# Low parts of weights all on VectorE, the down-sampled norms and most output copies on ScalarE

## The chip, the cores and the metric

The kernel runs on one core of a Trainium2 chip. The metric is the device time of one execution in microseconds (us). Times of the kernel before: 1001.62 us median of 3 runs (1001.51 to 1006.58). The profiled execution, from which all durations below come, took 1001.4 us, of which 999.3 us lie between its first and its last instruction (the span). Engines are named as the profile names them: PE is TensorE (PEld its weight loads), DVE VectorE, ACT ScalarE, POOL GpSimd, SP the engine that issues most DMAs.

## The reference

Attention on 4 batches of 8 heads, 576 positions, 64 wide, and behind it two feed-forward stages on all 2304 positions (tokens) of width 512:

```
q_d, k_d, v_d = means over 4 neighbours of q, k, v          # 144 positions per head
out_up        = repeat(softmax(q_d k_d^T / 8) v_d, 4)       # the down-sampled branch
out_local     = softmax(q k^T / 8 where |i-j| < 4) v        # a window of 7 positions
x = (out_up + out_local) as [2304, 512]
x = (silu(x @ w_gate) * (x @ w_val)) @ w_out                # 512 -> 1536 -> 512
h = x @ w_in;  x = (h * clip(h + 3, 0, 6) / 6) @ w_out2     # 512 -> 2048 -> 512
```

The weights arrive as 64-bit numbers. Products are made from two parts of each factor, a high part (the value rounded to PE's fp32r format) and a low part (what the rounding left): high by high, low by high and high by low are summed.

## The kernel before

**Blocks.** The 2304 tokens are cut into five blocks of 8, 6, 8, 8 and 6 units of 64 tokens (512 or 384 columns); they are called block 0 to 4. Each block runs through 68 weight tiles of 128x512, called units too: first, in the G half, 12 of `w_gate` (PSUM tile pG), 12 of `w_val` (pV) and 12 of `w_out` (aO), in the order G0 G1 V0 V1 G2 G3 V2 V3 O0 O1 G4 ...; then, in the H half, 16 of `w_in` (pH) and 16 of the second `w_out` (aP), two and two. A unit of G, V or H is 12 matmuls (4 row tiles by 3 products).

**Weights.** Block 0 loads each tile from the input, puts the 64-bit number together and writes it back to a scratch tensor `kept`; the later blocks load pairs of tiles from `kept` (w<-kept, three buffers). `split_unit` then makes the two parts of a tile, two units ahead of the unit that PE works on, into one of four `wr` buffers: ACT copies the high part (line 228), and line 231 subtracts it from the weight. That subtraction is on DVE, except in block 1, where every fourth tile's is on POOL (`POOL_SPLIT`, 17 tiles).

**Attention beside it.** Batch 0 is done ahead of the blocks. For batches 1 to 3 it is spread over the blocks: in the G half of block bi the window scores of chunks (DVE, lines 781 and 784, 2 us each), in the H half the window values (lines 818 to 824), whose result PE transposes (px, line 838) and DVE adds to the down-sampled branch (line 847). The down-sampled branch of batch bi+1 is made in blocks 0 to 2: POOL sums four neighbours (line 290 the first addition, line 291 the second, into the tiles dnq, dnk, dnv: four sums each, of half the positions by half the heads), PE transposes dnq and dnk (pqT and pkT, line 303, copied by ACT on line 314), and in the H half `down_main` goes through the heads: scores on PE (pS), maximum on DVE (line 697), exponential with its sum on ACT (line 701), the norm in `norm_d` (lines 707 to 709, all on DVE), a transpose on PE (pPT, line 715), a copy on ACT, the product with the values on PE (pO, line 722).

**What sets the order.** Each engine runs its own instructions strictly in the order of its list; semaphores make it wait where an operand comes from another engine. The lists are made by a scheduler when the program is built: it starts from the order of the program text and from its own idea of what each instruction takes, and puts forward what it believes to be ready. The only fixed order is that of instructions marked `keep_in_program_order`. So a change of an engine or of an operation can move other instructions too. The input DMAs and the output DMAs all stand in SP's one list.

**Outputs.** At the end of a block `put_out` copies each finished 128x512 tile of aP out of PSUM, the even ones on ACT (line 1014), the odd ones on DVE (line 1012), and SP sends it off (line 1023).

Of the kernel before, what the change touches and what calls it, by code (L numbers as in the profile page):

```python
# [10 lines left out]
F32 = mybir.dt.float32  # L11
# [6 lines left out]
AF = mybir.ActivationFunctionType  # L18
ALU = mybir.AluOpType
# [14 lines left out]
CLOAD = (0, 4)  # L34

EARLY = 6

POOL_SPLIT = {1: 4}


@with_exitstack
def tile_kernel(
# [12 lines left out]
    nc = tc.nc  # L55
# [6 lines left out]
    NJ = S // 4  # L62
    NJH = NJ // 2
# [10 lines left out]
    NB = len(BLOCKS)  # L74
# [44 lines left out]
    def flat(ap, off, dims):  # L119
        return bass.AP(ap.tensor, ap.offset + off, dims)  # L120
# [7 lines left out]
    def behind(ins):  # L128

        if front[0]:  # L130
            tc.keep_in_program_order(ins)
# [5 lines left out]
    units = []  # L137
# [20 lines left out]
    def view(t, i):  # L158
        return t[:, i % 2, :].rearrange("p (c e) -> p c e", c=NC)
# [65 lines left out]
    def split_unit(i):  # L225
        s = view(w32[i // 2], i)
        r = sp.tile([P, 2, NC, P], F32R, tag="wr", name=f"wr{i}", bufs=4)
        behind(nc.scalar.activation(r[:, 0], s, AF.Copy))  # L228
        n = POOL_SPLIT.get(units[i][2])
        eng = nc.gpsimd if n and i % n == 0 else nc.vector  # L230
        behind(eng.tensor_tensor(r[:, 1], s, r[:, 0].bitcast(F32), op=ALU.subtract))  # L231
        split[i] = r

    def prefetch(i):
        steps = ((LR, load_raw), (LD, load_kept), (LA, decode_a), (LB, decode_b), (LS, split_unit))
        for ahead, fn in steps:
            if 0 <= i + ahead < len(units):
                fn(i + ahead)
# [467 lines left out]
    def norm_d(pd, sd):  # L706
        nc.vector.tensor_scalar(sd, sd, EPS, 4.0, op0=ALU.add, op1=ALU.mult)
        nc.vector.reciprocal(sd, sd)
        nc.vector.tensor_tensor(pd, pd, sd[:, :, None].to_broadcast([NJH, 2, NJ]), op=ALU.mult)

    def trans_d(pd, ps):
        pt = ps[:NJH, :2 * NJ].rearrange("p (g j) -> p g j", g=2)
# [292 lines left out]
    def put_out(bi, e, ps):  # L1005
        if e == 0:

            done = sp.tile([P, NC, 2, UMAX * UT], F32R, tag="x2", name=f"os{bi}", bufs=1).bitcast(F32)
            state["os"] = done.rearrange("p c a t -> p (c a t)")
        os = state["os"][:, e * DM:(e + 1) * DM]  # L1010
        if e % 2:
            nc.vector.tensor_copy(os, ps)
        else:
            nc.scalar.activation(os, ps, AF.Copy)
        gu = starts[bi] + 2 * e
        (b, u), (b1, _) = divmod(gu, NG), divmod(gu + 1, NG)
        for n, m in ((0, 2),) if b == b1 else ((0, 1), (1, 1)):
            b, u = divmod(gu + n, NG)
            if b == 0:
                dst = out[(gu + n) * UT:(gu + n + m) * UT, :]  # L1020
            else:
                dst = flat(out, (b * S + u * 4) * DM, [[DM, 4 * m], [SL * DM, NSEG], [1, DM]])
            nc.sync.dma_start(dst, os[n * UT:(n + m) * UT, :])
# [115 lines left out]
```

## Time and profile before

| | before |
|---|---|
| median of 3 runs | 1001.62 us |
| the profiled execution | 1001.4 us, span 999.3 us |
| PE busy | 955.3 us (96%) |
| DVE busy | 787.6 us (79%) |
| ACT busy | 510.6 us (51%) |
| POOL busy | 137.2 us (14%) |

The five blocks begin at 72.8, 274.1, 453.4, 660.0 and 849.8 us of the span. How to read the rows further below: a row of a group of instructions gives line, engine, operation, tile written <- tiles read, shape, count, then busy time and mean duration in ns, then the idle time of that engine just before them and who ended it. A row of the timeline gives start and length in us. Two instructions of one engine can overlap a little, so that the distance of two starts (the pitch) is somewhat less than the duration. In the rows by stage (windows) each engine's busy time in the stretch is followed by its count, and PEclk is the granted clock of PE: 1.00 is 2.4 GHz, 0.50 would be 1.2 GHz throughout.

### The profile page before, as it was taken

The numbers are of one execution on the slowest core, as the hardware profiler recorded it, in microseconds if no ns is written. First come the engines' busy times: TensorE is split into PE (matmuls) and PEld (weight loads), VectorE is DVE, ScalarE is ACT, GpSimd is POOL, SyncE is SP. The second block draws the span as 40 slices with busy tenths as digits, with TensorE's granted clock in tenths as the row PEclk, the third lists the DMA queues.
The fourth block names the chain that finished last, engine by engine and source line by source line (L and its number), as shares of the span: only waits on it lengthen the run. The fifth ranks groups of instructions, "written<-read, shape, count | busy, mean of one in ns | idle before, by whom it ended". The sixth has DMA issues, their size and how long they took to land.

```text
span 999.3 us, 13482 instructions
## 1 busy us (share of the span) xinstructions
PE 955.3 (96%) x4800; PEld 796.1 (80%) x4800; DVE 787.6 (79%) x1251; ACT 510.6 (51%) x1058; POOL 137.2 (14%) x130
## 2 busy tenths in 40 slices
PE   8769999999998999879999999999999999999997
PEld 5658888778797987767878777788888788999996
DVE  6698986899999879998985699999346995545653
ACT  4667566766543475444333654443335444544653
POOL 5680000000068211103630000000000000000000
PEclk9789999999999999999999999999999999999999
DMA  9979999377677532245753212354322233533331
GB/s 194 211 222 318 304 321 319 115 248 262 222 238 219 179 107 80 85 148 164 222 172 115 76 64 93 124 191 141 104 85 90 85 100 111 157 125 124 124 123 50
DMA packets 83655, 160.72 MB, mean 161 GB/s; under 512 B 19460, under 2 KB 51716, under 8 KB 83588
## 3 DMA queue, kind: packets, MB, share of 16 engines
q1 hardware_dynamic: 78692, 142.03, 45.4%
q10 hardware_dynamic: 4896, 17.83, 5.1%
q8 instruction: 38, 0.62, 0.3%
q14 instruction: 29, 0.24, 0.1%
HBM read 137.29 MB, written 22.54 MB: 160 GB/s over the span
## 4 chain that ended last, share of the span: by engine, by line
PE 78%; DVE 14%; ACT 2%; issue 2%; DMA 2%; SPq 0%; ACTq 0%; DVEq 0%
PE aP L989 19%; PE pH L947 19%; PE aO L989 13%; PE pG L947 12%; PE pV L947 11%; DVE wr L231 3%; DVE pr L781 2%; DVE sc L784 1%; PE pS L872 1%; DVE gV L965 1%; ACT held L561 1%; PE pO L722 1%; DMA w<-kept 1%; DVE sl L959 1%; DMA w<-in_moe_w_val_dram 1%
## 5 line engine op out<-in xcount | busy, mean ns | idle before, releaser
L231 DVE TENSOR_TENSOR wr<-w,wr 128x512 fp32r<-128x512 f32 x323 | 235.1, 731 | 106.3 <-ACT wr L228 104.7
L228 ACT ACTIVATE wr<-w 128x512 fp32r<-128x512 f32 x340 | 212.1, 626 | 170.5 <-PE aP L989 58.7
L947 PE MATMUL pH<-x,wr 128*128 128x512 f32 (+1 forms) x960 | 217.2, 376 | 4.2 <-DVE wr L231 4.2
L989 PE MATMUL aP<-wr,gH 128*128 128x512 f32 x864 | 216.9, 400 | 0.7 <-DVE wr L231 0.7
L947 PEld LDWEIGHTS pH<-x,wr 128*128 128x128 f32 x960 | 173.6, 188 | 33.0 <-DVE wr L231 5.5
L989 PEld LDWEIGHTS aP<-wr,gH 128*128 128x128 f32 x864 | 160.5, 189 | 38.4 <-issue 2.3
L947 PE MATMUL pG<-xr,wr 128*128 128x512 f32 (+3 forms) x732 | 158.9, 371 | 10.8 <-ACT xr L265 4.2
L989 PE MATMUL aO<-gV,wr 128*128 128x512 f32 (+1 forms) x720 | 157.8, 375 | 2.9 <-DVE wr L231 2.9
L947 PEld LDWEIGHTS pG<-xr,wr 128*128 128x128 f32 x732 | 133.9, 192 | 30.4 <-ACT xr L265 4.3
L947 PE MATMUL pV<-xr,wr 128*128 128x512 f32 (+1 forms) x720 | 153.1, 368 | 0.0
L989 PEld LDWEIGHTS aO<-gV,wr 128*128 128x128 f32 x720 | 132.8, 190 | 22.7 <-DVE wr L231 3.6
L947 PEld LDWEIGHTS pV<-xr,wr 128*128 128x128 f32 x720 | 131.0, 188 | 16.7
L962 ACT ACTIVATE h<-pH,half 128x512 f32<-128x512 f32 (+1 forms) x80 | 51.6, 645 | 75.8 <-PE pH L947 75.5
L963 DVE SCALAR_TENSOR_TENSOR h<-h,pH 128x512 f32<-128x512 f32 (+1 forms) x80 | 50.4, 631 | 25.1 <-ACT h L962 24.0
L953 ACT ACTIVATE sl<-pG 128x512 f32<-128x512 f32 (+1 forms) x60 | 33.2, 554 | 64.6 <-PE pG L947 64.3
L964 ACT ACTIVATE gV<-sl 128x512 fp32r<-128x512 f32 (+1 forms) x60 | 35.2, 587 | 57.5 <-DVE sl L959 56.8
L781 DVE TENSOR_TENSOR pr<-q,k 128x1792 f32<-128x1792 f32 x27 | 58.8, 2178 | 6.7 <-DMA k<-in_k_dram 6.7
L231 POOL TENSOR_TENSOR wr<-w,wr 128x512 fp32r<-128x512 f32 x17 | 23.2, 1363 | 288.6 <-DVE h L963 195.2
L208 ACT ACTIVATE top<-w 128x512 f16<-128x512 bf16 x68 | 53.0, 790 | 10.4 <-DMA w<-in_moe_w_in_dram 4.0
L964 ACT ACTIVATE gH<-h 128x512 fp32r<-128x512 f32 (+1 forms) x80 | 46.9, 587 | 19.3 <-DVE h L963 17.3
L965 DVE TENSOR_TENSOR gH<-h,gH 128x512 fp32r<-128x512 f32 (+1 forms) x80 | 51.9, 650 | 3.6 <-ACT gH L964 2.6
L818 DVE TENSOR_TENSOR pv<-sc,v 128x1792 f32<-128x1792 f32 x27 | 54.5, 2018 | 0.2
(128 smaller groups left out, 825.1 us busy)
## 6 DMA issues: line engine op xcount, KB each, us to landing
w<-kept SPq DMA_DIRECT2D x136, 512.0 KB
kept<-w ACTq DMA_DIRECT2D x34, 512.0 KB
w<-in_moe_w_out_dram SPq DMA_DIRECT2D x28, 512.0 KB
w<-in_moe_w_in_dram SPq DMA_DIRECT2D x16, 512.0 KB
w<-in_moe_w_gate_dram SPq DMA_DIRECT2D x12, 512.0 KB
w<-in_moe_w_val_dram SPq DMA_DIRECT2D x12, 512.0 KB
out_dram<-os SPq DMA_DIRECT2D x16, 256.0 KB
nq<-in_q_dram SPq DMA_DIRECT2D x12, 288.0 KB
```

The source lines that it names most:

```text
L208: behind(nc.scalar.activation(halves(top[i % 2], 2, F16)[:, :, 1], h3.bitcast(BF16), AF.Copy))
L228: behind(nc.scalar.activation(r[:, 0], s, AF.Copy))
L231: behind(eng.tensor_tensor(r[:, 1], s, r[:, 0].bitcast(F32), op=ALU.subtract))
L781: nc.vector.tensor_tensor(pr, qt[:, a:a + SUB, None, :].to_broadcast([P, SUB, W, D]), win(kt, a, SUB), op=ALU.mult)
L818: nc.vector.tensor_tensor(pr, pe[:, a:a + SUB, :, None].to_broadcast([P, SUB, W, D]), win(vt, a, SUB), op=ALU.mult)
L947: nc.tensor.matmul(ps[:, cs], r[:, a, c], x[:, c, b_, cs], start=part is HIGH and a == c == 0, stop=part is LOW and c == NC - 1,)
L953: nc.scalar.activation(sl, ps, AF.Silu)
L962: nc.scalar.activation(h, ps, AF.Relu, scale=1 / 6, bias=half1[:, 0:1])
L963: nc.vector.scalar_tensor_tensor(h, h, 1.0, ps, op0=ALU.min, op1=ALU.mult)
L964: nc.scalar.activation(g[:, 0, :nt], h, AF.Copy)
L965: nc.vector.tensor_tensor(g[:, 1, :nt], h, g[:, 0, :nt].bitcast(F32), op=ALU.subtract)
L989: nc.tensor.matmul(ps, **one, start=f_ == 0 and a == b_ == 0, stop=f_ == nf - 1 and b_ == 1,)
```

## The change

POOL no longer makes any low part; `norm_d` keeps the two small operations on the sums on DVE and lets ACT multiply, in two instructions per head, one for each half of the positions; ACT copies all outputs, except that in the last block the odd ones stay on DVE.

```
-POOL_SPLIT = {1: 4}
...
-        n = POOL_SPLIT.get(units[i][2])
-        eng = nc.gpsimd if n and i % n == 0 else nc.vector
-        behind(eng.tensor_tensor(r[:, 1], s, r[:, 0].bitcast(F32), op=ALU.subtract))
+        behind(nc.vector.tensor_tensor(r[:, 1], s, r[:, 0].bitcast(F32), op=ALU.subtract))
...
         nc.vector.reciprocal(sd, sd)
-        nc.vector.tensor_tensor(pd, pd, sd[:, :, None].to_broadcast([NJH, 2, NJ]), op=ALU.mult)
+        for half in range(2):
+            nc.scalar.activation(pd[:, half], pd[:, half], AF.Copy, scale=sd[:, half:half + 1])
...
-        if e % 2:
+        if e % 2 and bi == NB - 1:
             nc.vector.tensor_copy(os, ps)
```

In the lists, POOL loses 17 instructions, all in block 1. Here is POOL's list at the start of block 1, before (names carry the program's numbers: wr72 is the buffer of tile 72, nq2_00 the q input of batch 2, first half of the positions and of the heads):

```order
L231 TENSOR_TENSOR wr68_2797<-w32_68_2706,wr68_2797 128x512
L290 TENSOR_TENSOR nq2_00_2877<-nq2_00_2877 72x4x128
L291 TENSOR_TENSOR dnq2_2874<-nq2_00_2877 72x256
L231 TENSOR_TENSOR wr72_2887<-w32_72_2795,wr72_2887 128x512
L290 TENSOR_TENSOR nq2_01_2879<-nq2_01_2879 72x4x128
L291 TENSOR_TENSOR dnq2_2874<-nq2_01_2879 72x256
```

and now (line numbers are 3 or 4 lower):

```order
L286 TENSOR_TENSOR nq2_00_2885<-nq2_00_2885 72x4x128
L287 TENSOR_TENSOR dnq2_2882<-nq2_00_2885 72x256
L286 TENSOR_TENSOR nq2_01_2887<-nq2_01_2887 72x4x128
L287 TENSOR_TENSOR dnq2_2882<-nq2_01_2887 72x256
L286 TENSOR_TENSOR nq2_10_2891<-nq2_10_2891 72x4x128
```

The sums of the down-sampled inputs now stand on POOL with nothing between them. The second place is PE's list at the start of block 2, before (pG2_2 is G2 of block 2, pqT3_0 the first transposes of dnq for batch 3):

```order
L947 MATMUL pV2_1_4651<-xr2_3832,wr139_4597 128x512 x12
L947 MATMUL pG2_2_4683<-xr2_3832,wr140_4628 128x512 x12
L947 MATMUL pG2_3_4705<-xr2_3832,wr141_4648 128x512 x12
L947 MATMUL pV2_2_4729<-xr2_3832,wr142_4674 128x512 x12
L947 MATMUL pV2_3_4749<-xr2_3832,wr143_4702 128x512 x12
```

and now:

```order
L944 MATMUL pV2_1_4667<-xr2_3844,wr139_4613 128x512 x12
L944 MATMUL pG2_2_4699<-xr2_3844,wr140_4644 128x512 x12
L299 MATMUL pqT3_0_5186<-ident_96,dnq3_4631 128x72 x4
L944 MATMUL pG2_3_4721<-xr2_3844,wr141_4664 128x512 x12
L944 MATMUL pV2_2_4745<-xr2_3844,wr142_4690 128x512 x12
```

The four transposes of pqT3_0, which stood 252 matmuls later, between V7 and O4 (units of block 2), now stand behind G2. They read the first and the third of the four sums in dnq. All other small PE groups (pS, pPT, pO, px, the other pqT and pkT) have moved by 12 matmuls at most. The third place is ACT's list at the start of block 1's H half, before (pd2_0 is the softmax tile of batch 2, head 0; h1_1, gH1_1 the activation of unit H1; wr109 the tile of unit P1, which is the second of aP):

```order
L701 ACTIVATE pd2_1_3719,sd2_1_3720<-pS2_1_3684,nm2_1_3717 72x144 x2
L964 ACTIVATE gH1_1_3705<-h1_1_3706 128x384
L228 ACTIVATE wr109_3777<-w32_108_3614 128x512
L962 ACTIVATE h1_2_3754<-pH1_2_3740,half1_101 128x384
```

and now:

```order
L697 ACTIVATE pd2_1_3727,sd2_1_3728<-pS2_1_3692,nm2_1_3725 72x144 x2
L961 ACTIVATE gH1_1_3713<-h1_1_3714 128x384
L706 ACTIVATE pd2_0_3721<-pd2_0_3721,sd2_0_3722 72x144 x2
L706 ACTIVATE pd2_1_3727<-pd2_1_3727,sd2_1_3728 72x144 x2
L959 ACTIVATE h1_2_3764<-pH1_2_3750,half1_101 128x384
L697 ACTIVATE pd2_2_3771,sd2_2_3772<-pS2_2_3731,nm2_2_3769 72x144 x2
L697 ACTIVATE pd2_3_3777,sd2_3_3778<-pS2_3_3732,nm2_3_3775 72x144
L961 ACTIVATE gH1_2_3763<-h1_2_3764 128x384
L697 ACTIVATE pd2_3_3777,sd2_3_3778<-pS2_3_3732,nm2_3_3775 72x144
L706 ACTIVATE pd2_2_3771<-pd2_2_3771,sd2_2_3772 72x144 x2
L706 ACTIVATE pd2_3_3777<-pd2_3_3777,sd2_3_3778 72x144 x2
L226 ACTIVATE wr109_3789<-w32_108_3622 128x512
```

The new norms (line 706) stand directly behind the exponentials, and the high part of wr109 has moved behind four exponentials and eight norms.

## Rows read from the trace of the kernel before

**Rows 1.** The page: the span, and part 1, PE.

```profile
span 999.3 us, 13482 instructions
...
PE 955.3 (96%) x4800; PEld 796.1 (80%) x4800; DVE 787.6 (79%) x1251; ACT 510.6 (51%) x1058; POOL 137.2 (14%) x130
```

**Rows 2.** Windows of half blocks; columns us, PE, PEld, DVE, ACT, POOL, PEclk, DMA, GB/s.

```profile
274.10:359.10 85.00, 78.86 (x450) 77.63 (x449) 75.79 (x80) 36.09 (x69) 44.24 (x33) 0.98 0.65 207
359.10:453.40 94.30, 84.56 (x451) 68.82 (x450) 88.83 (x180) 50.42 (x124) 9.52 (x7) 0.98 0.30 100
453.40:557.80 104.40, 101.58 (x449) 81.76 (x448) 81.60 (x88) 39.46 (x69) 32.92 (x24) 1.00 0.54 165
557.80:660.00 102.20, 102.15 (x498) 78.78 (x497) 96.14 (x184) 54.63 (x124) 0.00 (x0) 1.00 0.29 97
660.00:758.90 98.90, 98.90 (x433) 81.06 (x433) 62.46 (x79) 39.13 (x65) 0.00 (x0) 1.00 0.38 125
758.90:849.80 90.90, 90.90 (x398) 73.16 (x397) 74.84 (x128) 44.40 (x77) 0.00 (x0) 1.00 0.29 95
849.80:925.10 75.30, 75.30 (x434) 75.30 (x433) 39.32 (x64) 35.35 (x65) 0.00 (x0) 1.00 0.43 138
```

**Rows 3.** Groups by line, POOL, 266 to 453 us: the low parts in block 1.

```profile
L231 POOL TENSOR_TENSOR wr<-w,wr 128x512 fp32r<-128x512 f32 x17 | 23.2, 1363 | 288.6 <-DVE h L963 195.2 <-ACT wr L228 79.4 <-PE pPT L715 14.0
```

**Rows 4.** Timeline of POOL, block 1, H half.

```profile
374.01 1.30 POOL L231 TENSOR_TENSOR wr<-w,wr 128x512 fp32r<-128x512 f32 x1 [10.26 <-ACT wr L228]
```

**Rows 5.** Timeline of DVE, block 1: two low parts; a norm of sc.

```profile
343.69 1.28 DVE L231 TENSOR_TENSOR wr<-w,wr 128x512 fp32r<-128x512 f32 x2
...
374.23 1.15 DVE L813 TENSOR_TENSOR sc<-sc,sm 128x56 f32<-128x56 f32 x1
```

**Rows 6.** Groups by line and form, DVE, 359 to 453 us.

```profile
L231 DVE TENSOR_TENSOR wr<-w,wr 128x512 fp32r<-128x512 f32 x25 | 18.0, 723 | 0.2 <-ACT wr L228 0.2
...
L965 DVE TENSOR_TENSOR gH<-h,gH 128x384 fp32r<-128x384 f32 x16 | 10.2, 634 | 0.2
...
L823 DVE TENSOR_TENSOR pv<-pv 128x512 f32<-128x512 f32 x8 | 6.1, 761 | 0.0
L709 DVE TENSOR_TENSOR pd<-pd,sd 72x288 f32<-72x288 f32 x8 | 3.6, 444 | 0.0
...
L813 DVE TENSOR_TENSOR sc<-sc,sm 128x56 f32<-128x56 f32 x4 | 2.9, 716 | 0.0
```

**Rows 7.** The same view, block 4 (850 to 999 us): gH without POOL.

```profile
L965 DVE TENSOR_TENSOR gH<-h,gH 128x384 fp32r<-128x384 f32 x16 | 8.9, 558 | 0.0
```

**Rows 8.** Same view, block 2 (557 to 660 us): sc without POOL.

```profile
L813 DVE TENSOR_TENSOR sc<-sc,sm 128x56 f32<-128x56 f32 x1 | 0.2, 208 | 0.0
```

**Rows 9.** Timeline of PE, block 1, G half: a wait for POOL, one for DVE.

```profile
311.36 4.28 PE L947 MATMUL pG<-xr,wr 128*128 128x384 f32 x23 [2.06 <-POOL wr L231]
...
324.95 3.59 PE L989 MATMUL aO<-gV,wr 128*128 128x384 f32 x11 [2.86 <-DVE wr L231]
```

**Rows 10.** Windows: PE behind the wait that ends at 324.95 us.

```profile
326.00:329.00 3.00, 3.00 (x13) 0.66 0.96 327
```

**Rows 11.** Timeline of SP, start of block 2: the first inputs of batch 3.

```profile
457.02 2.09 SPq L124 DMA_DIRECT2D nq<-in_q_dram  x2
```

**Rows 12.** Timeline of POOL, start of block 2: the third sum of dnq.

```profile
473.75 1.07 POOL L291 TENSOR_TENSOR dnq<-nq 72x256 f32<-72x256 f32 x1
```

**Rows 13.** Timeline of PE, start of block 2: G2, then G3.

```profile
464.00 2.88 PE L947 MATMUL pG<-xr,wr 128*128 128x512 f32 x12
468.98 2.97 PE L947 MATMUL pG<-xr,wr 128*128 128x512 f32 x12 [2.10 <-DVE sl L959]
```

**Rows 14.** Chain of waits, 430 to 560 us: the first pqT of block 2.

```profile
528.93 0.25 PE pqT L303 x4
```

**Rows 15.** Groups by line, ACT: its nearest row to a norm of one half.

```profile
L463 ACT ACTIVATE qdT<-tmp 128x144 f32<-128x144 f32 x4 | 1.3, 321 | 0.9 <-DVE tmp L460 0.8
```

**Rows 16.** Timeline of DVE, block 0: between two steps of a norm.

```profile
194.38 2.01 DVE L818 TENSOR_TENSOR pv<-sc,v 128x1792 f32<-128x1792 f32 x1
```

## The prediction

> **What bounds the kernel now.** I read the page first, then the stages, then who waits, then the lists. PE is busy for 955.3 of 999.3 us [rows 1], so at most 44 us can go without taking work from PE. The windows by half block [rows 2] (block 1 G and H, block 2 G and H, block 3 G and H, block 4 G) say where the rest is. In block 3 and in block 4's G half PE has no idle time at all, though DVE has a good deal (62.46 of 98.90 us busy): nothing that DVE gives up there moves the end. Block 2's H half is the same to 0.1 us of PE (102.15 of 102.20), although DVE is at 94%. Block 1 is the exception: PE is idle for 6.1 us of its G half (85.00 - 78.86) and 9.7 us of its H half (94.30 - 84.56), while DVE is busy for 75.8 of 85.0 and 88.8 of 94.3 us. There DVE sets the pace. Block 2's G half sits between: PE idles 2.8 us (104.40 - 101.58), and it takes 5.5 us more than block 3's, which has the same matmuls. So an edit counts where it changes DVE's load in block 1, or makes PE wait anywhere.
>
> **Low parts from POOL to DVE.** Seventeen subtractions of 1.36 us leave POOL [rows 3], seven of them in block 1's H half (POOL x7 in [rows 2]) and ten before. DVE pays for each not its 0.68 us duration but its pitch: two in a row take 1.28 us [rows 5], so the second costs 0.60. That is 17 x 0.60 = 10.2 us more for DVE. But POOL's work was not free to DVE. A norm of sc, which takes 0.21 us where POOL rests [rows 8], took 1.15 at 374.23 us and ended at 375.38 [rows 5], just behind POOL's subtraction, which ended at 375.31 [rows 4]. In block 1's H half POOL does nothing but these seven, so the lengthening of DVE's rows there is their price: low parts 25 x (0.723 - 0.68) = 1.1, gH 16 x (0.634 - 0.558) = 1.2, line 823 (as large as a low part) 8 x (0.761 - 0.68) = 0.6, sc 4 x (0.716 - 0.208) = 2.0, together 5.0 us or 0.71 each [rows 6 to 8]. Against 0.60 that is a relief of 0.11 each: 0.8 us in the H half, 1.1 in the G half. So the move costs DVE nothing, where a count of busy time would say 10 us.
>
> The Trainium skill ("SBUF — State Buffer", section "SBUF: two separate sides") says that GpSimd and a VectorE instruction with two SBUF inputs take a shared port pair exclusively for a whole instruction. The end of the sc norm agrees. Were DVE shut out for all of each subtraction, 1.36 us, the relief would be 17 x 0.76 = 12.9 instead of 1.9 us, and the forecast 11 us lower; I keep the rows' 0.71, since DVE's reductions and its reads of PSUM go on.
>
> **Norms and output copies.** Per block 0 to 2, eight multiplications of 0.44 us [rows 6] leave DVE, at the same overlap 0.36 each, 2.9 us. In blocks 0 and 2 PE is the bound and they buy nothing; in block 1's H half they count. Of the seven copies that leave DVE two stand at the start of block 1's G half, 2 x 0.60 = 1.2 us; the others lie beside a full PE.
>
> **Block 1, summed.** H half: relief 0.8 + 2.9 = 3.7 us. If DVE stays as full as it is, 94.3 x (88.8 - 3.7) / 88.8 = 90.4, 3.9 us less; I take 3.5, because ACT's part below is in the way. G half: relief 1.1 + 1.2 = 2.3 us, and PE's wait for a POOL subtraction that stood behind a sum, 2.06 us [rows 9], ends with its cause: 4.4. The wait of 2.86 us for DVE [rows 9] would be shorter too. Behind it PE's granted clock was 0.66 [rows 10], a mixture of 1.2 and 2.4 GHz, and 11 matmuls took 3.59 us where 23 of the same shape take 4.28 [rows 9]: 3.59 - 11 x 0.186 = 1.5 us for the fallen clock. I count hardly any of that: 4.5. Block 1 together: -8.0, with -3 as the least (POOL's wait and 1 us more) and -14 as the most (G's whole idle time, its 1.5 us, and two thirds of H's).
>
> **Block 2: the transposes that moved.** The new list has PE do the first pqT behind G2. In the run before they were done at 528.93 us [rows 14], long after their sums. Now PE comes to them when G2 ends, 464.00 + 2.88 = 466.9 [rows 13], but the third sum, which they need, ends at 473.75 + 1.07 = 474.8 [rows 12]. It cannot come much sooner: SP sends for q at 457.02 [rows 11], behind block 1's outputs, in an order that the change leaves alone here, and moves with the end of block 1. With the transposes' 0.25 us [rows 14] G3 starts at 475.1 instead of 468.98 [rows 13], where it already waited 2.10 for DVE: +6.1. Everything behind stands in PE's list and waits too. After 8 us without work I add the fallen clock of [rows 10], +1.5. Something comes back: of the 5.5 us over block 3, 2.1 are that old wait and 1.0 the four groups of transposes; the other 2.4 are later waits for DVE, which can run ahead while PE stands. I take 1.6 of them back. Block 2: 6.1 + 1.5 - 1.6 = +6.0, between +5.2 (all 2.4 back) and +7.6 (none).
>
> The skill ("TensorE: Matmul & The Clock Gate", section "HAM oscillation — how this bites in real kernels") says that a wait lets the clock fall, so that the work after it starts slow. [Rows 10] agree. Without it the forecast would be 1.5 us lower.
>
> **ACT.** It gains 48 norms and 7 copies. Its nearest row is a scaled copy of 144 columns, 0.32 us [rows 15], so 16 x 0.32 = 5.1 us per H half. ACT is busy for 50.4 of 94.3 and 54.6 of 102.2 us there [rows 2]: the work fits, but the queue matters. A norm waits for DVE's reciprocal, and behind it stand the activation of the next pH unit and high parts of weights. In block 1 the high part of P1's tile now stands behind eight norms, 8 x 0.32 = 2.6 us later, and PE wants it one unit after P0. I take +1.0, between 0 (all hidden by the two units of lead) and 7.8 (2.6 in each of three H halves).
>
> **Sum.** -8.0 + 6.0 + 1.0 = -1.0 against the profiled execution's 1001.4: 1000.4 us. The median of the runs, 1001.62, is 0.2 above that execution.
>
> **Rivals.**
> - *Block 1 gains much more.* For it: DVE is full there, PE's idle time is 15.8 us, and each wait may also cost clock. Against it: DVE's relief is only 6 us. With -14: 1001.4 - 14 + 6 + 1 = 994.4.
> - *The transposes do not wait, or PE's wait is not missed,* because DVE is the bound there. Against it: PE has only 2.8 us of idle time in that half, and after the wait it still has all its matmuls to do. Then block 2 is 0: 994.4.
> - *ACT becomes the queue that all wait for* (the slower side). Between two steps of a norm DVE does a product of 2.01 us [rows 16]; a norm on ACT would stand that long, and the weights behind it. Over 12 pairs of heads, with 0.8 us of it reaching PE each time, 9.6 in place of 1.0: 1001.4 - 8 + 6 + 9.6 = 1009.0. It decides from about 0.6 us a pair. Against it: high parts are made two units ahead, and most weights are not behind a norm.
>
> **How the numbers follow.** Forecast 0.56, block 1 gains more 0.18, no loss in block 2 0.09, ACT 0.17. A measurement of this kernel can tell some 0.5% (5 us) from no change. So faster by over 0.5% 0.27, within 0.56, slower 0.17. The likeliest case's own range is 996.5 to 1006; taking in the others until 2 in 10 are left out, and the bounds -14 + 5.2 + 0 = -8.8 and -3 + 7.6 + 2.6 = +7.2, gives 993.5 to 1007.5.
>
> **What would show it.** Right: PE's timeline in block 2 has one wait of 7 to 8 us for POOL's dnq ahead of the first pqT, and slow matmuls behind it; DVE's gH, sc and line 823 in block 1's H half are back at 0.56, 0.21 and 0.68 us; block 1's halves take some 80.5 and 91 us; blocks 3 and 4 are as before. Wrong: no such wait; block 1 as long as before, which would mean that DVE's load was not its bound; or ACT's norms idle before by more than a microsecond each, with PE's waits for wr behind them.

## The result and the profile after

The changed kernel takes 1009.2 us (median of 9 runs, 1006.46 to 1012.5), the kernel before 1002.3 us (median of 9, 1001.0 to 1006.58): ratio 1.0058, 95% interval 1.0041 to 1.0075. It is slower by 0.6%. The forecast was 1000.4 us, in a range of 993.5 to 1007.5, so the measured time lies above the range. The profiled execution took 1007.28 us; its page:

```profile
span 1005.5 us, 13513 instructions
...
PE 958.6 (95%) x4797; PEld 800.2 (80%) x4800; DVE 772.7 (77%) x1237; ACT 526.3 (52%) x1113; POOL 112.5 (11%) x113
```

DVE has 14.9 us less to do than before and the span is 6.2 us longer. The windows of the half blocks (block 1 G and H, block 2 G and H, block 3 G and H, block 4 G; columns as in [rows 2]) say where:

```profile
275.20:356.60 81.40, 78.04 (x449) 75.97 (x449) 72.28 (x87) 36.28 (x69) 31.27 (x24) 1.00 0.69 217
356.60:452.70 96.10, 87.12 (x452) 72.11 (x451) 87.06 (x179) 55.28 (x141) 0.00 (x0) 0.95 0.30 100
452.70:563.30 110.60, 102.40 (x448) 83.45 (x447) 78.19 (x86) 40.40 (x70) 31.73 (x24) 0.95 0.50 154
563.30:666.60 103.30, 103.19 (x498) 79.08 (x497) 93.69 (x176) 59.53 (x141) 0.00 (x0) 1.00 0.29 96
666.60:765.40 98.80, 98.80 (x433) 80.95 (x432) 61.78 (x79) 39.50 (x66) 0.00 (x0) 1.00 0.37 124
765.40:856.30 90.90, 90.90 (x398) 73.19 (x397) 74.23 (x128) 45.00 (x78) 0.00 (x0) 1.00 0.29 95
856.30:931.60 75.30, 75.30 (x434) 75.30 (x433) 38.69 (x63) 35.82 (x66) 0.00 (x0) 1.00 0.41 138
```

Against [rows 2]: block 1's G half 3.6 us less (forecast 4.5 less), its H half 1.8 more (forecast 3.5 less), block 2's G half 6.2 more (forecast 6.0 more), its H half 1.1 more (forecast, as ACT's term, 1.0 more). Blocks 3 and 4 are as before, to 0.1 us a half. One term failed by much, that of block 1's H half.

Block 2 went as worked out, but that the one wait of 7 to 8 us came as two, 8.2 us together. PE's timeline from G2 on:

```profile
463.00 2.88 PE L944 MATMUL pG<-xr,wr 128*128 128x512 f32 x12
468.70 0.28 PE L299 MATMUL pqT<-ident,dnq 72*128 72x72 f32 x1 [2.82 <-POOL dnq L287]
474.36 0.62 PE L299 MATMUL pqT<-ident,dnq 72*128 72x72 f32 x3 [5.38 <-POOL dnq L287]
474.73 5.23 PE L944 MATMUL pG<-xr,wr 128*128 128x512 f32 x12
```

and POOL's third sum of dnq, for which the longer wait stands:

```profile
473.59 0.72 POOL L287 TENSOR_TENSOR dnq<-nq 72x256 f32<-72x256 f32 x1
```

The third sum ends at 474.31 (worked out: 474.8) and G3 starts at 474.73 (475.1). G3 then takes 5.23 us where it took 2.97 [rows 13]: 2.3 us for the clock, where I had put 1.5. The granted clock in that stretch is a mixture of 2.4 and mostly 1.2 GHz:

```profile
474.70:480.00 5.30, 5.30 (x16) 4.20 (x15) 2.03 (x1) 0.41 (x1) 2.00 (x2) 0.54 1.03 353
```

DVE's rows in block 1's H half came back to the lengths that they have when POOL rests, as expected (0.558, 0.68 and 0.208 us in [rows 5 to 8]):

```profile
L227 DVE TENSOR_TENSOR wr<-w,wr 128x512 fp32r<-128x512 f32 x32 | 21.6, 679 | 1.5 <-ACT wr L226 1.5
L962 DVE TENSOR_TENSOR gH<-h,gH 128x384 fp32r<-128x384 f32 x16 | 8.8, 552 | 1.1 <-ACT gH L961 1.0
L820 DVE TENSOR_TENSOR pv<-pv 128x512 f32<-128x512 f32 x8 | 5.5, 682 | 0.0
L810 DVE TENSOR_TENSOR sc<-sc,sm 128x56 f32<-128x56 f32 x4 | 0.8, 210 | 0.0
```

So DVE was relieved, and block 1's H half, which the prediction had paced by DVE, still became longer.

### The profile page after: what moved, and what is told of

Read it like the earlier page. It is cut to its first block, busy times and chain, and to the rows that moved or that the text cites. A ratio compares the mean times of both kernels' runs of the same rounds, so it can differ in the third digit from the quotient of the medians.

```text
span 1005.5 us, 13513 instructions
## 1 busy us (share of the span) xinstructions
PE 958.6 (95%) x4797; PEld 800.2 (80%) x4800; DVE 772.7 (77%) x1237; ACT 526.3 (52%) x1113; POOL 112.5 (11%) x113
## 4 chain that ended last, share of the span: by engine, by line
PE 66%; issue 14%; DMA 3%; POOL 3%; DVE 2%; ACT 0%; ACTq 0%; POOLq 0%
PE pH L944 16%; PE aP L986 16%; PE aO L986 11%; PE pV L944 10%; PE pG L944 10%; DMA nk<-in_k_dram 1%; DMA nv<-in_v_dram 1%; POOL nq L286 1%; PE pS L869 1%; DMA nq<-in_q_dram 1%; PE pO L719 1%; POOL dnq L287 0%; PE px L835 0%; PE pPT L712 0%; POOL nv L286 0%
## 5 line engine op out<-in xcount | busy, mean ns | idle before, releaser
L227 DVE TENSOR_TENSOR wr<-w,wr 128x512 fp32r<-128x512 f32 x340 | 240.7, 712 | 115.7 <-ACT wr L226 114.0
L944 PE MATMUL pG<-xr,wr 128*128 128x512 f32 (+3 forms) x732 | 161.4, 375 | 4.5 <-ACT xr L261 4.0
L944 PEld LDWEIGHTS pG<-xr,wr 128*128 128x128 f32 x732 | 136.8, 196 | 23.1 <-ACT xr L261 4.2
L778 DVE TENSOR_TENSOR pr<-q,k 128x1792 f32<-128x1792 f32 x27 | 56.2, 2080 | 8.7 <-DMA k<-in_k_dram 8.6
L286 POOL TENSOR_TENSOR nq<-nq 72x512 f32<-72x512 f32 x12 | 18.9, 1574 | 354.8 <-PE pV L944 210.1
L215 DVE SCALAR_TENSOR_TENSOR w<-w,top 128x512 int32<-128x512 int32 x68 | 48.6, 722 | 9.8 <-ACT top L206 9.4
```

What stands on the lines that cost most here:

```text
L215: behind(nc.vector.scalar_tensor_tensor(w32[i // 2][:, i % 2].bitcast(I32), h12, 13, top[i % 2], op0=ALU.logical_shift_right, op1=ALU.bitw ...
L227: behind(nc.vector.tensor_tensor(r[:, 1], s, r[:, 0].bitcast(F32), op=ALU.subtract))
L778: nc.vector.tensor_tensor(pr, qt[:, a:a + SUB, None, :].to_broadcast([P, SUB, W, D]), win(kt, a, SUB), op=ALU.mult)
L944: nc.tensor.matmul(ps[:, cs], r[:, a, c], x[:, c, b_, cs], start=part is HIGH and a == c == 0, stop=part is LOW and c == NC - 1,)
```

## The experiments

All times by stage below are read from one profile of each kernel, from the first matmul of a half to the last of the half's last unit; "clock" is the mean granted clock of block 1's H half. Taken in this way, stages differ by 0.1 to 0.3 us from the windows above, which end where the next half begins. Ratios are to the kernel before, timed on the same chip.

| kernel | ratio, 95% | G 1 | H 1 | clock | G 2 | H 2 |
|---|---|---|---|---|---|---|
| before | | 84.9 | 94.5 | 0.98 | 104.1 | 102.3 |
| before_again | | 86.0 | 94.4 | 0.98 | 105.3 | 102.4 |
| after | 1.0058 (1.0041 to 1.0075) | 81.4 | 96.2 | 0.95 | 110.5 | 103.3 |
| after_again | | 81.6 | 96.1 | 0.95 | 110.4 | 103.3 |
| late | 0.9996 (0.9979 to 1.0013) | 82.3 | 96.1 | 0.95 | 104.8 | 103.3 |
| split | 0.9954 (0.9936 to 0.9973) | 79.9 | 95.9 | 0.96 | 105.2 | 102.3 |
| split_again | 0.9980 (0.9963 to 0.9996) | 82.4 | 98.3 | 0.93 | 104.2 | 102.4 |
| split_outs | 0.9995 (0.9979 to 1.0011) | 84.1 | 97.1 | 0.95 | 106.0 | 102.3 |
| so_cload | 1.0011 (0.9995 to 1.0026) | 82.6 | 94.5 | 0.98 | 107.9 | 102.3 |
| split_norm_late | 1.0014 (0.9999 to 1.0028) | 84.8 | 96.6 | 0.93 | 106.2 | 103.4 |
| norm | 1.0034 (1.0019 to 1.0050) | 82.2 | 96.2 | 0.98 | 106.1 | 103.3 |
| outs | 1.0030 (1.0014 to 1.0047) | 87.6 | 95.6 | 0.96 | 103.1 | 102.3 |
| late_light | | 82.8 | 93.3 | 0.95 | 105.8 | 103.8 |
| late_o | 1.0019 (1.0004 to 1.0033) | 81.8 | 99.6 | 0.91 | 105.2 | 103.3 |
| late_o2 | 1.0015 (0.9993 to 1.0037) | 83.1 | 99.9 | 0.91 | 106.4 | 103.3 |
| late_x | 0.9997 (0.9980 to 1.0013) | 82.4 | 95.8 | 0.95 | 105.6 | 103.4 |
| split_ls3 | 1.0004 (0.9984 to 1.0023) | 81.4 | 96.6 | 0.96 | 104.6 | 102.2 |
| split_poolq | 1.0120 (1.0092 to 1.0149) | 76.4 | 107.7 | 0.92 | 99.7 | 102.2 |
| split_g | 0.9946 (0.9928 to 0.9964) | 81.1 | 94.3 | 0.98 | 104.9 | 102.3 |

### Block 2: the transposes

**late.** In `sums_T`:

```
-nc.tensor.transpose(pt[...], dn[w][...], ident[:NJH, :NJH])
+ins = nc.tensor.transpose(pt[...], dn[w][...], ident[:NJH, :NJH])
+if b == B - 1:
+    tc.keep_in_program_order(ins)
```

> The changed kernel with one thing put back: the first transposes of block 2 (pqT3_0) are pinned to their place in the program, behind V9 of block 2; nothing else in any list moves but their copy on ACT. Theory A (the wait of these transposes costs what the trace after shows in block 2's G half: 110.7 us instead of 104.3): PE has no wait between G2 and G3 but the old one of some 2 us, the clock does not fall there, block 2's G half takes 104 +- 1 us, and the time falls by 6.4 to 1002.8 (1001.5 to 1004). Theory B (block 2 is paced by something else that the norms on ACT or the fuller DVE bring, and the wait only stands where that shows first): the wait reappears behind G3 or V2 and the time falls by less than 2.5, to 1006.7 or more. Block 1's H half has the same lists as after: if its 96.0 us are a matter of the lists, it takes 96 +- 0.7 again, with clock falls at the same three places; if they are chance, it can be 92 as well.

Measured 1003.98 us, ratio 0.9996 where the changed kernel has 1.0058: 6.2 us less, theory A. Between G2 and G3 only the old wait for DVE is left, 2.61 us (2.10 in [rows 13]):

```profile
463.43 2.88 PE L946 MATMUL pG<-xr,wr 128*128 128x512 f32 x12
468.92 4.58 PE L946 MATMUL pG<-xr,wr 128*128 128x512 f32 x12 [2.61 <-DVE sl L958]
```

Behind it G3 was slow here too, 4.58 us, which theory A had excluded; the half still took 104.8. Block 1's H half takes 96.1 again.

### Which edit does what

**split**, **norm** and **outs** each make one of the three edits on the kernel before; **split_outs** and **split_norm_late** two (the latter with the pin of late). Their diffs are the three pieces of the change.

> The kernel before with one edit: all low parts on DVE; norms and output copies as before. Differs from the run with the output copies only by who copies 8 of the 18 output tiles that are not the last block's. Theory A (relief of 1.9 us from POOL plus the wait for POOL's subtraction): G half of block 1 82 to 83 (two copies stay on DVE: 1.2 us less relief than after), H half 93 to 94; time 999.5 (998 to 1001). If low parts on DVE cost what their duration says (17 x 0.60 = 10.2 us in a block where DVE is full): block 1 5 to 10 us longer, time 1007 to 1012.

> The kernel before with one edit: the norm's product on ACT; low parts on POOL in block 1, odd outputs on DVE as before. pqT3_0 stays late. Theory A (norms on ACT cost more in waits than they free on DVE): block 1's H half 95 to 97 instead of 94.3, block 2's H half 103.2 as after; time 1003.5 to 1006. Theory B (DVE's load sets block 1's H half: 8 x 0.36 = 2.9 us less): H half 91 to 92, time 999 to 1000.5. Theory C (ACT's place in the lists is hidden and DVE is no bound): within 1 us of 1002.3.

> The kernel before with one edit: the output copies of blocks 0 to 3 all on ACT; low parts and norms as before. In the lists hardly anything moves but the copies and, on SP, the outputs against the first nq loads. Theory A (the order on SP is the cost, whoever makes low parts): G half of block 1 86 to 89 instead of 84.9, with a wait of DVE for k of 3 us or more; ratio 1.002 to 1.005. Theory B (two copies less on DVE, nothing else): ratio 0.998 to 1.0005.

> The changed kernel with the norm put back on DVE (one product of 72x288 per head); low parts on DVE and the output copies on ACT stay. In its lists pqT3_0 stands late, as before. Theory A (norms on ACT spoil block 1's H half; DVE's relief from POOL is real): G half of block 1 81.6 us as after, H half 94.3 - 0.8 to 94.3 - 3, so 91 to 93.5, block 2 as before; time 1002.3 - 3.4 - 2 = 997 (995 to 998.5). Theory B (block 1's H half is a loop of waits, unit to activation to low part to unit, that DVE's load does not set): H half 94.5 to 96.5, G half 81.6; time 999 to 1001. Theory C (the move of the low parts is worth nothing, and the G half's gain is chance): G half 84 to 85, time 1001.5 to 1003.

> Low parts on DVE and norms on ACT, output copies as before; the first transposes of block 2 pinned to their place in the program, so that their wait stays out. Theory A (the edits add up): 0.9954 and 1.0034 give 0.9988, 1003.1 where before is 1004.3; block 1's H half 96 us, block 2's H half 103.3. Theory B (the norms cost only what they cost in the H half of block 2, 1.0 us, and their cost of 3.4 us in the run of norms alone comes from meeting POOL's subtractions): 0.996 to 0.997. Theory C (norms on ACT are what keeps block 1 from gaining): 1.000 to 1.003.

Low parts on DVE are the good edit (0.9954), against the count of busy time, which says 10 us worse; in the profile the gain lies in the G half (79.9), while the H half is longer, against theory A. How much of it is POOL's absence is less sure than that number: norm, where POOL keeps its subtractions, has a G half of 82.2 too, and PE still waits 1.8 us for one of them. The other two are harmful on their own, each by its theory A: norm 1.0034, with 96.2 and 103.3 us in the H halves, outs 1.0030, with 87.6 in the G half. Split and outs together give 0.9995 (G half 84.1, as theory C has it, H half 97.1, beyond all three), split and norm 1.0014 (theory C, by a little), all three without the transposes' wait 0.9996. The products of the single ratios are 0.9984, 0.9988 and 1.0018, each uncertain by some 0.0025 to 0.003; that the edits help or hinder each other is not shown by these.

For the output copies the trace of split_outs shows how they can cost time. At the start of block 1 SP's list now has all outputs ahead of the first nq loads; the third nq load waits for POOL's first sum, and k stands behind it. SP, then DVE and PE:

```profile
277.02 0.94 SPq L122 DMA_DIRECT2D nq<-in_q_dram  x2
278.73 0.35 SPq L174 DMA_DIRECT2D w<-kept  x1
286.41 3.01 SPq L122 DMA_DIRECT2D nq<-in_q_dram  x2
289.51 0.36 SPq L174 DMA_DIRECT2D w<-kept  x1
289.92 0.42 SPq L122 DMA_DIRECT2D q<-in_q_dram  x1
290.39 0.42 SPq L122 DMA_DIRECT2D k<-in_k_dram  x1
```

```profile
296.46 2.02 DVE L777 TENSOR_TENSOR pr<-q,k 128x1792 f32<-128x1792 f32 x1 [5.33 <-DMA k<-in_k_dram]
298.40 0.55 DVE L961 TENSOR_TENSOR gV<-sl,gV 128x384 fp32r<-128x384 f32 x1
298.87 0.55 DVE L955 TENSOR_TENSOR sl<-sl,pV 128x384 f32<-128x384 f32 x1
299.33 1.29 DVE L227 TENSOR_TENSOR wr<-w,wr 128x512 fp32r<-128x512 f32 x2
...
300.08 1.33 PE L943 MATMUL pG<-xr,wr 128*128 128x384 f32 x3 [3.06 <-DVE wr L227]
```

The product waits 5.33 us for k, the low parts stand behind it, and PE waits 3.06 us for one of them. In outs alone DVE's waits for k are 3.5 us (1.1 before).

**so_cload** takes that cause away: `CLOAD = (0, 4)` becomes `(0, 1)`.

> Low parts on DVE and output copies on ACT (the run that took 0.9995 of before, against 0.9954 without the output copies), with one constant changed: the second chunk's q, k and v of a block are asked for two units after its start instead of five, so that they stand ahead of the nq loads in SP's list and not behind the third and fourth, which wait for POOL's sums. Theory A (the output copies cost time because SP sends the outputs ahead of the first nq loads, so POOL's first sum is late, SP stands at the third nq load, and k behind it is late for DVE's products, which stand ahead of a low part that PE waits for): DVE's wait of 5.3 us for k in block 1's G half and PE's wait of 3.1 us behind it are gone, no clock fall there, G half 80 to 81.5 us instead of 84.1; ratio to before 0.994 to 0.997. Theory B (ACT's two more copies, or the output copies' place in ACT's list, are the cost): PE's wait in the G half stays within 1 us, ratio 0.998 to 1.001.

DVE's wait for k fell to 0.5 us and PE's 3.06 us went, so the link is right; but the G half fell only to 82.6, block 2's G half rose to 107.9 (ACT there waited 15.5 us for kept weights, 5.2 in split_outs), and the ratio is 1.0011. Theory A's time failed. One load put ahead seems to have made others late; that was not tested.

**split_poolq** (on split: `down_sums(db, dn, qk, nat_tile, 2, nc.gpsimd)`) frees SP altogether.

> Low parts on DVE, all else as before, with the down-sampled inputs (nq, nk, nv of batches 2 and 3) loaded from POOL's own queue instead of SP's, so that SP does not stand at a load that waits for POOL's sums. The scheduler then puts the sums and all transposes of block 2 into block 1's H half. If SP's standing is what makes inputs late in the G halves: block 1's G half 78 to 80 and block 2's G half 99 to 103 instead of 79.9 and 105.2, ratio 0.988 to 0.993. Against it, POOL's 24 sums then fall into the H half, where DVE has two-input operations that they hold up (some 0.7 us each in the subtractions of the kernel before), and the transposes can make PE wait: H half 97 to 105, ratio 0.996 to 1.005.

PE has no idle time left in block 1's G half:

```profile
287.40:363.80 76.40, 76.40 (x449) 76.27 (x448) 67.27 (x89) 36.57 (x69) 9.83 (x10) 1.00 0.61 196
363.80:471.50 107.70, 93.06 (x467) 75.06 (x467) 98.65 (x187) 52.67 (x128) 23.13 (x22) 0.92 0.34 108
```

but POOL's sums now lie in the halves where DVE is full: the H half takes 107.7 us, and block 0's halves 108.2 and 106.7 (100.0 and 101.5 before). 1.0120.

### Block 1's H half

**before_again** and **after_again** are the two kernels unchanged.

> The kernel before, unchanged, for a second profile: its runs lie between 1000.8 and 1010.7 us, and the profiled execution (1001.4) is at the low end. If block 1 is decided by the lists, its G and H halves take 84.9 and 94.5 us again to 0.5 us, with the clock falling at the same two places, and the difference lies in the stretch ahead of block 0 and in its first 100 us, where inputs stream in; if block 1's waits are chance, its H half takes between 93 and 97, as in the kernels run so far (95.9 to 97.1), and the 94.5 of the first profile was a lucky one.

> The changed kernel once more, for a second profile. If the waits are set by the lists, block 1's H half shows the same waits of PE to 0.1 us (1.95, 3.68 and 2.55) and takes 95.5 to 97.5, by how often the clock falls behind them; block 2's G half takes 109.5 to 111.5 with two waits for the sums of 2.5 to 3 and 5 to 6 us; block 0's G half 100 to 102.

The H half is the same thing each time: 94.5 and 94.4 before, 96.2 and 96.1 after, PE's long waits 2.75 and 2.74, 2.95 and 2.93 before, 1.95, 3.68 and 2.55 after and 1.95, 3.69 and 2.59 again. late has these waits once more, and 96.1. The waits are the lists'. That the 1.7 us are so too is likely, with two profiles before and three after (and split_g, further down, with the waits of before and 94.3), but not certain: two profiles of split have the same waits and take 95.9 and 98.3. (Block 1's G half does not repeat so well: 84.9 and 86.0 before.) Cut at the first product of the window values (line 815, 818 before) and at the end of the last of them, it shows where. Before, then after:

```profile
359.00:375.40 16.40, 16.34 (x94) 13.28 (x93) 13.93 (x35) 13.11 (x39) 2.59 (x2) 1.00 0.28 92
375.40:447.70 72.30, 62.78 (x340) 51.29 (x338) 70.22 (x135) 35.53 (x82) 6.93 (x5) 1.00 0.31 104
447.70:453.50 5.80, 5.64 (x19) 4.46 (x20) 4.88 (x12) 1.88 (x4) 0.00 (x0) 0.72 0.25 86
```

```profile
356.60:373.70 17.10, 17.04 (x99) 14.26 (x98) 11.99 (x33) 15.91 (x48) 0.00 (x0) 1.00 0.20 65
373.70:444.20 70.50, 61.84 (x326) 51.39 (x324) 67.50 (x136) 36.24 (x88) 0.00 (x0) 0.95 0.31 105
444.20:452.70 8.50, 8.23 (x29) 6.46 (x30) 7.57 (x14) 3.13 (x6) 0.00 (x0) 0.80 0.42 132
```

In the first stretch PE is full and DVE idle for 2.5 us before (16.40 - 13.93) and 5.1 after: 1.9 us of DVE's relief fall where nothing waits for it. The stretch is 0.7 us longer, because the window values need ACT's exponential of sc (line 795), and ACT, now busy for 15.91 of 17.10 us, comes to it 15.1 us after the start of the half (372.73 - 359.0 = 13.7 before), behind four norms:

```profile
367.82 1.43 ACT L706 ACTIVATE pd<-pd,sd 72x144 f32<-72x144 f32 x4
...
371.66 0.66 ACT L795 ACTIVATE sc<-sc 128x56 f32<-128x56 f32 x4
```

In the middle DVE is full (70.22 of 72.30); there 2.7 us of relief give 1.8. In the last stretch, behind the last window values, PE has 29 matmuls to do instead of 19: 2.7 us. 0.7 - 1.8 + 2.7 = 1.6.

Read for PE, the same rows say what the 1.6 us consist of. PE's idle time fell only from 9.7 us (94.5 less the sum of its busy times) to 9.0, and its busy time rose by 2.4, from 84.8 to 87.1, with one matmul more (453 and 454). What rose is the time at the lower clock. Before, PE's clock fell in one place, at the last of the long waits, and not behind the wait of 2.75 us that ends at 428.68 (first two rows); after, it fell behind each of the three (last three rows), 0.57 being a mixture of 1.2 and 2.4 GHz:

```profile
428.70:432.70 4.00, 4.00 (x24) 3.90 (x25) 3.87 (x12) 1.53 (x4) 0.00 (x0) 1.00 0.36 131
447.00:451.00 4.00, 3.14 (x8) 2.43 (x9) 3.69 (x10) 0.94 (x2) 0.00 (x0) 0.57 0.01 4
```

```profile
387.00:391.00 4.00, 4.00 (x17) 3.04 (x15) 2.13 (x6) 1.76 (x6) 0.00 (x0) 0.57 0.38 134
428.00:432.00 4.00, 4.00 (x14) 3.66 (x13) 3.92 (x13) 2.04 (x4) 0.00 (x0) 0.57 0.32 121
445.00:449.00 4.00, 4.00 (x11) 3.13 (x12) 3.54 (x9) 1.46 (x3) 0.00 (x0) 0.57 0.44 135
```

Two of the three falls lie in the middle stretch (clock 0.95 instead of 1.00). There PE does 14 matmuls fewer, five of which it had done in the first stretch; the others stand behind the last window values.

**late_light** leaves out two of the three positions that line 819 adds, and so two of the seven positions of the window: `pr[:, :, 0:1] += pr[:, :, 3:4]` in place of `0:3` and `3:6`, on late.

> The changed kernel with the first transposes of block 2 pinned late, and with a part of the computation left out: the first of the three additions of the window values takes one position (256 columns) instead of three (768), so two of the seven positions are missing from the result; 0.6 us less per unit of the window values, 4.8 us less for DVE in block 1's H half (87.1 us busy without it). The scheduler moves some instructions by up to 26 places. Theory A (PE's waits in that half come from what stands ahead in the lists, not from DVE's load): H half 94 to 96.5 instead of 96.1, DVE's idle time grows by most of the 4.8. Theory B (DVE's load sets the half, as the prediction assumed): H half 96.1 - 4.8 x 0.9, so 91 to 92.5. Blocks 0, 2 and 3 the same to 0.5 us either way, since PE is full there.

DVE's busy time fell by 4.5 us (87.1 to 82.6), the half by 2.8 (96.1 to 93.3), PE's idle time from 9.0 to 6.2, while its clock stayed at 0.95. Neither theory: what is taken from DVE in its full stretch comes through by about 0.6.

**late_o** and **late_o2** move what PE waits with at 29 us of the half (pO, 1.95 us), on late. `first_o` are the four matmuls of pO2_0, in late_o2 the eight transposes behind them too; `mm` is a matmul of H6:

```
+for ins in first_o:
+    tc.add_manual_dep(ins.ins, mm.ins.name, ...)
```

> The changed kernel with the first transposes of block 2 pinned late and, besides, the first product with the values in block 1's H half (pO2_0) pinned behind the eighth matmul of unit H6; in the changed kernel it stands directly behind the second scores (pS2_4, pS2_5), before there were seven matmuls of H6 between. Theory A (PE's wait of 1.95 us at 28.9 us of that half is pO2_0 waiting for the bank of pS2_4, which ACT's exponentials read: a list effect of the moved norms, with a clock fall of 1.7 us behind it): that wait is gone, the rest of the half's idle time is 6.5 to 8.5 us, H half 92 to 95 instead of 96.1, ratio to before 0.994 to 0.9975 where the run with the transposes alone took 0.9996. Theory B (DVE's values are what is late, as the trace names them): the wait shows again at the next transposes or at pO2_0 in its new place, H half 95.5 to 97, ratio 0.999 to 1.001.

> As the run before it, with the transposes that then took the first product's place (pPT2_2 and pPT2_3) pinned behind the same eighth matmul of H6, so that nothing that needs the banks of the scores pS2_4 and pS2_5 stands directly behind them in PE's list. Theory A (what waits is the bank, held by the scores until ACT's exponentials have read them, and so a matter of PE's list): no wait above 0.7 us between 27 and 40 us of block 1's H half (1.95 with the transposes alone pinned, 2.62 + 0.52 with the product pinned), and no clock fall there; the waits of 1.8 and 3.6 us at 73 and 93 us stay, H half 93 to 96 and by the number of falls; ratio 0.996 to 0.999. Theory B (DVE's backlog at that place holds PE whatever stands next): a wait of 1.5 us or more for a low part or for the norm shows between 27 and 40 us, H half 96 to 99, ratio 1.000 to 1.002.

The wait did not go, it took the next in PE's list. PE in late, late_o and late_o2:

```profile
385.93 0.72 PE L721 MATMUL pO<-pT,dnv 72*64 72x144 f32 x8 [1.95 <-DVE pv L822]
```

```profile
384.54 0.44 PE L714 MATMUL pPT<-ident,pd 72*72 72x72 f32 x4 [2.62 <-DVE sd L706]
```

```profile
386.18 0.69 PE L955 MATMUL pH<-x,wr 128*128 128x384 f32 x1 [2.55 <-DVE h L978]
```

Theory A (a held bank) fell twice; that it is DVE's backlog at that place fits both, though the halves became longer than theory B had them, 99.6 and 99.9, with the granted clock down to 0.91. The pins also changed the rest of the lists.

**late_x** pins the last transposes (px21) seven matmuls later, on late: `tc.add_manual_dep(px21, first matmul of the last unit of aP, ...)`.

> The changed kernel with the first transposes of block 2 pinned late and, besides, the last transposes of the window values in block 1 (px21) pinned seven matmuls later in PE's list, so that 17 matmuls of aP are left behind them; in the changed kernel 24 and two of G are left, in the kernel before 15 and one. Theory A (part of what DVE's relief brings is given back because PE stands at px21, which waits for DVE's last window values, with more work still behind it): PE's wait of 2.59 us at 87.7 us of the half falls to 0.5 to 1.2 us, no clock fall behind it, H half 93 to 95 instead of 96.1; ratio to before 0.9965 to 0.999 where the run with the transposes alone took 0.9996. Theory B (the half ends when DVE is done, wherever the wait stands): the wait moves to G0 of block 2, which needs what px21 gives, H half and the first 10 us of the next together as long as before, ratio 0.999 to 1.001.

The wait of 2.59 us at px became one of 3.13 us at aP, for a low part, at the same place of the half (88.2 us); H half 95.8. Theory B in effect.

**split_ls3** (on split: `LS = 3`, with the transposes pinned) makes low parts a unit earlier.

> Low parts on DVE, all else as before (the run that took 0.9954), with the two parts of a weight tile made three units ahead of the unit that PE works on instead of two, still in four buffers; the first transposes of blocks 1 and 2 are pinned to their place. In DVE's list of block 1's H half each low part stands some four operations earlier (that of tile 127 ahead of the window values of unit 18 and not between them). Theory A (that half is set by what stands in the lists ahead of the low part that PE waits for, not by DVE's load): PE's waits there for low parts, 1.84, 2.39 and 0.35 us, fall by 2 us or more together, H half 92 to 94.5 instead of 95.9, ratio to before 0.990 to 0.994. Theory B (DVE's load sets it): the same work in another order, waits of 9 to 10 us in all, H half 95 to 97, ratio 0.994 to 0.997. Theory C (with four buffers the high part then waits for PE to give a buffer free and holds up ACT's queue): waits for ACT or for low parts grow, ratio above 0.998.

H half 96.6, PE's idle time 10.3 us (9.5 in split): PE waits 9.2 us for low parts, 4.6 in split. Ratio 1.0004, theory C.

### A version that beats both

**split_again** repeats split.

> The kernel before with one edit, all low parts on DVE, once more: it was the fastest of the kernels so far (0.9954, 95% interval 0.9936 to 0.9973), chosen from many, so its next ratio is likely nearer to 1. If the gain is block 1's G half without POOL's subtractions (79.9 against 84.9 and 86.0 us): 0.995 to 0.998, with a G half of 79.5 to 82 and the waits of the H half the same to 0.1 us (1.14, 1.84, 2.39, 0.35, 3.63). If it was a lucky run: 0.999 to 1.001, G half 83 to 85.

0.9980: smaller than the first time, still below 1. The H half had the same waits and took 98.3.

**split_g** moves only the low parts of block 1's G half to DVE:

```
-eng = nc.gpsimd if n and i % n == 0 else nc.vector
+eng = nc.gpsimd if n and i % n == 0 and units[i][0] in "HP" else nc.vector
```

> The kernel before with low parts moved from POOL to DVE in block 1's G half only; in its H half POOL keeps its seven. PE's list is that of the kernel before. Theory A (what the move gives is the G half, where POOL's subtraction stands behind its sums and PE waited for it; in the H half the relief and the extra load of DVE cancel): G half 80 to 83 us instead of 84.9 and 86.0, H half with the waits of the kernel before to 0.1 us (0.67, 0.66, 0.72, 0.75, 2.75, 0.97, 2.94) and 94.4 to 97, by the clock; ratio 0.994 to 0.998. Theory B (the gain of the run with all low parts on DVE needs the H half too): G half above 83.5, ratio 0.998 to 1.001.

998.34 us, ratio 0.9946 (0.9928 to 0.9964): faster than the kernel before and, by its ratio, than the changed one. This is one measurement, and split's two differ by 0.0026. Theory A: the G half falls to 81.1, and the H half keeps the waits of the kernel before:

```profile
275.80:356.90 81.10, 78.17 (x450) 76.02 (x448) 74.26 (x88) 36.09 (x69) 34.55 (x25) 1.00 0.68 217
356.90:451.20 94.30, 84.67 (x451) 68.96 (x451) 88.98 (x180) 50.49 (x124) 9.57 (x7) 0.98 0.29 101
```

## Why the prediction was wrong

**The step that failed** is "If DVE stays as full as it is, 94.3 x (88.8 - 3.7) / 88.8 = 90.4, 3.9 us less; I take 3.5". It takes the half to shrink as DVE's load does. DVE's relief came (its busy time fell from 89.0 to 87.1 us, and 2.0 of the 87.1 are a product of block 2 that now stands at the end of the half), but DVE did not stay as full: its idle time rose from 5.5 to 9.0 us. PE shows what became of the relief. Its idle time, which the relief was to shorten by 3.5 us, fell by 0.7, from 9.7 to 9.0. And its busy time rose by 2.4 us, because its clock fell behind three waits instead of at one: 0.95 in the mean instead of 0.98. This second part the prediction had put at nothing in this half, though it priced fallen clocks in block 1's G half and in block 2. The difference in clock is worth about as much in other profiles: with the same waits and 9.5 us of idle time, PE is busy for 85.1 us at 0.98 and 87.6 at 0.95 (so_cload and split_outs, in the last section). Forecast 3.5 less, measured 1.7 more: 5.2 us of the 6.8 between the forecast difference (-1.0) and the measured one (+5.8, from the ratio); block 1's G half makes 1.0 of the rest.

Of the relief 1.9 us lay in the first 17 us, where DVE waits anyway and PE is full, and ACT's norms delayed the start of the window values by 0.7. That the rise of 2.7 us at the end comes from the place of the last transposes in the list was tested by late_x and not borne out; it holds the matmuls that PE had not done before. Why the clock fell behind the new lists' waits of 1.95 and 3.68 us, and not behind the old one of 2.75, stays open.

**Block 1's G half** was forecast 4.5 less and is 3.5 less (84.9 to 81.4), or 4.4 between the second profiles. In the first profile PE's wait for POOL, 2.06 us, went with its cause. But the second profile of before shows no wait of PE for POOL in that half, and the half took 86.0 us, with waits for DVE instead (3.3 us in aO, 1.6 in pV, 1.8 in pG). So the term came out near its size, while the wait that nearly half of it was made of is there in one execution only. What split_g shows is that the half is shorter without POOL's subtractions, not through which wait. The order of SP's list at this boundary, where the outputs now stand ahead of the nq loads, was not in the sum at all.

**POOL's price to DVE** was sized right. From split, in DVE's full stretch (the row below, against the row 375.40:447.70 of the kernel before), five more low parts at 0.60 us and five fewer subtractions on POOL changed DVE's busy time from 70.22 to 69.77 us: (5 x 0.60 + 0.45) / 5 = 0.69 us each, where I took 0.71. If the rule of the Trainium skill ("SBUF — State Buffer", "SBUF: two separate sides": the pair of ports is held for a whole instruction) had cost DVE the full 1.36 us each time, DVE would have gained 3.8 us there and not 0.45. The measurement decides.

```profile
371.10:444.90 73.80, 64.58 (x341) 53.06 (x339) 69.77 (x140) 36.00 (x82) 0.00 (x0) 0.98 0.30 104
```

**Block 2's G half** was right: +6.0, measured +6.4 (104.1 to 110.5) and, between the second profiles, +5.1, and gone with the pin. Its parts: the wait as worked out, the clock 2.3 instead of 1.5, and 2.4 that come back instead of 1.6 (PE is 8.0 us behind at V2, 479.79 against 471.79, and 5.6 at the end of the half, 563.28 against 557.65).

**ACT** was right in size by luck. The 1.0 us were forecast for weights that PE would get late. Block 2's H half grew by 1.0 or a little more in every kernel with norms on ACT (103.3 to 103.8) and in none without (102.2 to 102.4), but not by a wait: PE's busy time grew, with no idle time and at a clock of 1.00. Why was not traced further. The rival's sign, norms that stand on ACT's queue for their operand, did not show: ACT was not idle before the 16 in block 1's H half.

```profile
L706 ACT ACTIVATE pd<-pd,sd 72x144 f32<-72x144 f32 x16 | 5.5, 414 | 0.0
```

In block 1 ACT's fuller queue cost 0.7 us in one place, at an exponential and not at a weight.

**The level.** The profiled execution of before, 1001.4 us, lies at the low end of what the kernel does: the medians on the same chips as the experiments were 1003.3 to 1004.3. The G halves and the prologue vary by one to 2.5 us from one execution to another (split's G half of block 1: 79.9 and 82.4).

## What to carry to other kernels

An engine that is 94% busy over a half is not the bound over all of it: cut the half where its work changes, and count a relief only in the stretch where the engine is full and something waits for it. Then ask of the engine that waits how much idle time the relief can take away, and price the clock behind each wait that stays: here 0.7 us less idle time and 2.4 us more for the lower clock. Price every move that the listing of the order shows on a queue that others stand in: 252 places of one small group cost 6 us, and outputs ahead of four loads let DVE wait 5.3 us for one behind them. When a change has several edits, try the one that takes an engine out of a conflict by itself, and only in the stage where the conflict is waited for: here a part of one of three edits was the fastest kernel measured.

## What was not expected of the hardware

The same waits cost different amounts. In four profiles, two of them of one kernel, PE's waits in block 1's H half are the same to 0.1 us (4.6 us for low parts, 3.6 for window values, 1.1 ahead of scores), and the half took 94.6, 95.9, 97.1 and 98.3 us. PE is idle for 9.5 us in each. The granted clock (first column behind POOL's) is what differs, more or less of the time at 1.2 GHz behind the same waits (so_cload, split, split_outs, split_again):

```profile
357.80:452.40 94.60, 85.09 (x452) 69.17 (x451) 89.11 (x188) 51.25 (x125) 0.00 (x0) 0.98 0.29 101
```

```profile
355.00:450.90 95.90, 86.42 (x452) 70.69 (x451) 88.44 (x187) 51.08 (x124) 0.00 (x0) 0.96 0.29 99
```

```profile
360.00:457.10 97.10, 87.61 (x452) 71.35 (x451) 89.94 (x188) 51.41 (x125) 0.00 (x0) 0.95 0.29 98
```

```profile
358.40:456.70 98.30, 88.84 (x451) 72.91 (x450) 88.30 (x187) 50.99 (x124) 0.00 (x0) 0.93 0.28 97
```

The Trainium skill ("TensorE: Matmul & The Clock Gate", "HAM oscillation — how this bites in real kernels") says that work behind a wait starts slow; the rows agree, and add that it does so in one execution and not in another.
